# Queries loaded two tokens to a partition and turned by 64x64 identity products: attention followed by a hierarchical mixture of experts

## The chip, the cores and the metric

The kernel runs on one core of a Trainium2 chip. A core has TensorE for matrix products, VectorE (DVE) and ScalarE (ACT) for elementwise work, GpSimd (POOL), and SyncE (SP), which here only issues transfers. Transfers are issued on the queues of SP, ACT and POOL and are carried out by 16 DMA engines. The metric is the device time of one execution in microseconds (us).

## The reference

Queries have 8 batches of 16 heads, 384 tokens and 64 dimensions; keys and values have one head per batch. Every token's attention output, 16 heads x 64, is a row of 1024 that goes to one expert out of 4 groups x 4 experts.

```python
scores = (1/8) * q @ k.T
attn = softmax(scores); attn_out = attn @ v          # [B, H, S, D]
x = attn_out.transpose(0, 2, 1, 3).reshape(B * S, H * D)
g_idx = argmax(x @ w_group); g_w = softmax(x @ w_group)[g_idx]
e_idx = argmax(x @ w_expert[g_idx]); e_w = softmax(...)[e_idx]
out = g_w * e_w * (relu(x @ w1[g_idx, e_idx]) @ w2[g_idx, e_idx])
```

## The kernel before

Attention is done in 24 pairs `p`, three for each batch: a pair is one batch and one stretch of 128 tokens, for all 16 heads. For a pair the queries must stand as `qT`, a tile of 128 partitions x 1024: partitions 64a to 64a + 63 hold the 64 dimensions of the heads 8a to 8a + 7, and the columns are those eight heads by 128 tokens. The keys of a batch stand as `kT`, dimensions on partitions (in both halves) by 384 keys.

Scores are made in six rounds `j` of 64 keys (`scores`, L251): four float32 products on 64x64 tiles of the array, rows 64a (head half) by columns 64c (which four heads of the half), each 512 columns wide. ScalarE takes the exponential of a round (L253), VectorE adds the six rounds up (`pre_add`, L259 and L261) and folds them (L265) for the sums over keys, and `values` (L290) multiplies the exponentials with the batch's values, again in six rounds on four tiles. `weigh` (L300) multiplies with the inverse sums and leaves `xT`. At pair 2 the gate products of batch 0 (`gate_a`, L312) read `xT` of pair 0 and the choice of expert weights follows. From pair 4 on, the products with the chosen experts (L407, L415) are put between the rounds of attention.

The order of all work on each engine is the order in which the program is written. An engine takes its instructions in that order, and waits for semaphores. A transfer that is issued as the ninth or later waits for the landing of an earlier one, since eight semaphores go round.

Most pairs get their `qT` from a block transpose on VectorE (`prep_q`, L243), for which the queries are loaded in 128-byte pieces. The first four pairs (batch 0, and the first stretch of batch 1) get it otherwise. Their queries are loaded in natural order (`load_first`, tiles `qn` and `qe`): token on the partition, for each head one piece of 64 numbers, 256 bytes. `turn_q` then transposes them on TensorE: eight transposes of 128x128, one for each head position, both head halves side by side, into the space `qps`, from where they are copied to `qT`. For pair 0 the eight are two lots of four with a space each: ScalarE copies the first lot, VectorE the second. Pair 1 is turned after the first round of scores of pair 0 and copied by VectorE; pair 2 in pair 1, pair 3 in pair 2, both copied by ScalarE. The keys of batch 0 are loaded twice side by side (tile `kn`, both on ACT's queue), and turned by three transposes (`turn_k_first`, L219).

Ahead of all that 48 products of ones (L152, L442) keep TensorE busy while the first loads are on their way.

The loads at the start, in the order of their queues. ACT: keys twice, one quarter of pair 0's queries, then the table load and a first exponential (L160). SP: three quarters of pair 0's queries (L127), pair 1's in two loads (L129), batch 1's keys in four (L107), batch 0's values in two (L113), pair 2's queries in two (L134), pair 3's in two (L138), ten loads of gate weights (L199, L201), and batch 1's other queries (L92).

Of the kernel before, what the change touches and what calls it, by code (L numbers as in the profile page):

```python
# [9 lines left out]
FP32 = mybir.dt.float32  # L10
# [3 lines left out]
P = 128  # L14
# [7 lines left out]
def kernel(  # L22
# [11 lines left out]
    nc = tc.nc  # L34
    B, H, S, D = q.shape
# [6 lines left out]
    ST = S // P  # L42
# [5 lines left out]
    CW = 512  # L48
# [10 lines left out]
    HP = H // 2  # L59
    HC = CW // P  # L60
    NB = S // 32
    NBP = 2 * CW // 32
    KB = S // D
# [7 lines left out]
    pool = fast.enter_context(tc.tile_pool(name="work", bufs=2))  # L71
# [4 lines left out]
    def side(shape, dtype, name):  # L76
        return ps_s.tile(shape, dtype, tag="s", name=name)

    q_raw, k_raw, v_sb, kT, qT, pt, xT, xbf, gsel, wts = {}, {}, {}, {}, {}, {}, {}, {}, {}, {}

    q_todo = []
    q_nat = []
# [20 lines left out]
    def load_k(b):  # L103
        kt = pool.tile([P, NB, 32], FP32, tag="k", bufs=2, name="k")
        for a in range(2):
            for j in range(2):
                nc.sync.dma_start(out=kt[64 * a + 32 * j:64 * a + 32 * j + 32], in_=kv[b, 0, j])  # L107
        k_raw[b] = kt

    def load_v(b):  # L110
        vt = pool.tile([P, KB, D], FP32, tag="v", name="v")
        for c in range(2):
            nc.sync.dma_start(out=vt[64 * c:64 * c + 64], in_=v[b, 0].rearrange("(j i) d -> i j d", j=KB))  # L113
        v_sb[b] = vt

    qn = q[0].rearrange("(a hp) (st p) d -> st p a hp d", a=2, p=P)
    kn = k[0, 0].rearrange("(st p) d -> p st d", p=P)

    def load_first():
        kt = pool.tile([P, ST, 2, D], FP32, tag="k", bufs=2, name="kn")  # L120
        qt = pool.tile([P, ST, HP, 2, D], FP32, tag="qraw", bufs=2, name="qn")
        for a in range(2):
            nc.scalar.dma_start(out=kt[:, :, a], in_=kn)
        for c in range(2):
            hs = slice(c * HC, (c + 1) * HC)
            for a in range(2):
                (nc.scalar if c and a else nc.sync).dma_start(out=qt[:, 0, hs, a], in_=qn[0, :, a, hs])  # L127
        for a in range(2):
            nc.sync.dma_start(out=qt[:, 1, :, a], in_=qn[1, :, a])  # L129
        k_raw[0], q_raw[0] = kt, qt  # L130
        load_k(1)
        load_v(0)
        for a in range(2):
            nc.sync.dma_start(out=qt[:, 2, :, a], in_=qn[2, :, a])  # L134
        qe_in = q[1].rearrange("(a hp) (st p) d -> st p a hp d", a=2, p=P)
        qe = pool.tile([P, HP, 2, D], FP32, tag="y", bufs=4, name="qe")
        for a in range(2):
            nc.sync.dma_start(out=qe[:, :, a], in_=qe_in[0, :, a])  # L138
        q_nat.append(qe)

    def load_w1(w1, e):
# [11 lines left out]
    ident = singles.tile([P, P], FP32, name="ident")  # L153
    make_identity(nc, ident)
    load_first()

    one = singles.tile([P, 1], FP32, name="one")
# [38 lines left out]
    def load_gw():  # L196
        for a in range(2):
            rows = slice(a * D, (a + 1) * D)
            nc.sync.dma_start(out=gw[rows, :, 0:G], in_=moe_w_group.rearrange("(a ko d) g -> a d ko g", a=2, d=D)[a])  # L199
            for g in range(G):  # L200
                nc.sync.dma_start(out=gw[rows, :, G + g * Eg:G + (g + 1) * Eg], in_=moe_w_expert[g].rearrange("(a ko d) e -> a d ko e", a=2, d=D)[a])  # L201
# [13 lines left out]
    def turn_k_first():  # L215
        kT[0] = pool.tile([P, S], FP32, tag="kT", name="kT")
        ps = side([P, CW], FP32, "kps")
        for st in range(ST):
            nc.tensor.transpose(out=ps[:, st * P:(st + 1) * P], in_=k_raw[0][:, st].rearrange("p a d -> p (a d)"), identity=ident[:])  # L219
        nc.vector.tensor_copy(out=kT[0][:], in_=ps[:, 0:S])  # L220

    def turn_q(p, nat, copies):
        qT[p] = pool.tile([P, 2 * CW], FP32, tag="qT", bufs=2, name="qT")
        n = HP // len(copies)
        for i, copy in enumerate(copies):
            ps = side([P, 2 * CW], FP32, "qps")
            for h in range(n):
                nc.tensor.transpose(out=ps[:, h * P:(h + 1) * P], in_=nat(i * n + h).rearrange("p a d -> p (a d)"), identity=ident[:])
            copy(out=qT[p][:, i * n * P:(i + 1) * n * P], in_=ps[:, 0:n * P])

    def prep_k(b):
        kT[b] = pool.tile([P, S], FP32, tag="kT", name="kT")
# [2 lines left out]
    def q_of(p):  # L235
        b, st = divmod(p, ST)
        if b == 0:
            return q_raw[0][:, st].rearrange("p h a d -> p h (a d)")
        return q_raw[b][:, :, st * (P // 32):(st + 1) * (P // 32)].rearrange("p h k d -> p h (k d)")

    def prep_q(p):
# [91 lines left out]
    def counts(now, full):  # L333
        n = GE * (1 + ST)
        ps = side([P, n], FP32, "cps")
        lo, hi = (0 if now is not None else GE), (n if full is not None else GE)
        if now is not None:
            nc.tensor.matmul(out=ps[:, 0:GE], lhsT=ones_bf[:], rhs=first[now][:].rearrange("p g e -> p (g e)"), start=True, stop=True)
        if full is not None:
            nc.tensor.matmul(out=ps[:, GE:n], lhsT=ones_bf[:], rhs=ohe_t[full][:].rearrange("p s g e -> p (s g e)"), start=True, stop=True)  # L340
        t = pool.tile([P, n], FP32, tag="cnt1", bufs=2, name="cnt1")
        nc.scalar.copy(out=t[:, lo:hi], in_=ps[:, lo:hi])
        if now is not None:
            seen[now] = t[:, 0:GE]
            choose_b(now, t[:, 0:GE])
        if full is not None:
            gate_c(full, t[:, GE:n])
# [93 lines left out]
    for _ in range(18):  # L441
        nc.tensor.matmul(out=warm[:, 0:P], lhsT=ones_bf[:], rhs=ones_bf[:], start=True, stop=True)  # L442
    turn_k_first()
    turn_q(0, lambda h: q_raw[0][:, 0, h], [nc.scalar.copy, nc.vector.tensor_copy])
    load_gw()

    units = []
# [18 lines left out]
    def gates(b):  # L466
        if b == 0:
            choose_a(0, gate_a(0, 0, 1))
            return
        ps = gate_a(b, 0, ST)  # L470
        choose_a(b, ps)
        gate_logits(b - 1, ps, 1, ST)
        gate_math(b - 1)
# [72 lines left out]
    for p in range(NP):  # L546
        b, st = divmod(p, ST)
        jobs = [lambda: gates(0), lambda: None, lambda: counts(0, None)] if p == 2 else []
        if p == 0 or p == ST or (st == 1 and 1 < b < B - 1):
            load_q(b + 1)  # L550
        for j in range(3):
            scores(p, j)
            if p == 0 and j == 0:
                turn_q(1, lambda h: q_raw[0][:, 1, h], [nc.vector.tensor_copy])
        if p == 0:
            stats_k(0)
            prep_k(1)
        elif p == ST:
            prep_q(p + 1)
        if jobs:  # L560
            jobs.pop(0)()
        for j in (1, 2):
            pre_add(p, j)
        for j in range(KB):
            if p > 0:
                values(p - 1, j)
            if j == 2 and p > 0:
                join(p - 1)
            if j + 3 < KB:
                scores(p, j + 3)  # L570
            if 0 < j < 4:
                pre_add(p, j + 2)
            if j == 2 and p > 0:
                invert(p - 1)
            if j == 3:
                stats_q(p)
                if p == 1:
                    turn_q(2, lambda h: q_raw[0][:, 2, h], [nc.scalar.copy])
                elif p == 2:
                    turn_q(3, lambda h: q_nat[0][:, h], [nc.scalar.copy])  # L580
            if jobs:
                jobs.pop(0)()
            if p == ST + 1 and j == 0:
                fill(3)
            if st == 1 and 0 < b < B - 1 and j == 0:
                load_k(b + 1)
            if 0 < j < 5:
                some_q(1 if p <= ST + 1 else 2)
            if st == 1 and b + 1 < B and j == KB - 1:
                load_v(b + 1)  # L590
        assert not jobs
        if p > 0:
            weigh(p - 1)
        fold_keys(p)
        if st == 2 and b + 1 < B:
            stats_k(b + 1)
        if p in PHASES:
            n = PHASES[p]
            steps = {}
            if st < 2:  # L600
                prep_q(p + 1)
            if st == 0:
                counts(None, b - 2)
            elif st == 1:
# [258 lines left out]
```

## Time and profile before

| | |
|---|---|
| median of 5 runs | 463.21 us (462.59 to 463.55) |
| the profiled execution | 462.79 us, its span 461.3 us |
| mean granted clock of TensorE | 0.993 |
| busy, share of the span | TensorE 98%, VectorE 66%, ScalarE 53%, GpSimd 13% |
| 128x128 transposes of the queries (L228) | 32, of 273 ns each at the median, in four lots of eight |
| their copies to `qT` (L229) | ScalarE 0.59 us (half a pair) and 1.00; VectorE 0.69 (half a pair) and 1.22 |
| loads of the natural queries, issue to landing | pair 0's quarters 2.9 to 4.4 us, pairs 1 and 2 some 5 us, pair 3 5.4 us |

The span runs from the first to the last instruction; the execution's time has some 1.5 us around it. In the views below a row of the timeline has the start and duration in us, the engine, the source line, what is written and read, how many instructions were merged, and in brackets how long the engine stood idle before and what ended that. PEld is TensorE's loading of weights, PE its products. The rows of a view by windows have, for each stretch, its length and the busy time of PE, PEld, DVE, ACT and POOL with the number of instructions, then the granted clock as a share, the DMA engines' busy share and GB/s.

### The profile page before, as it was taken

The numbers are of one execution on the slowest core, as the hardware profiler recorded it, in microseconds if no ns is written. First come the engines' busy times: TensorE is split into PE (matmuls) and PEld (weight loads), VectorE is DVE, ScalarE is ACT, GpSimd is POOL, SyncE is SP. The second block draws the span as 40 slices with busy tenths as digits, with TensorE's granted clock in tenths as the row PEclk, the third lists the DMA queues.
The fourth block names the chain that finished last, engine by engine and source line by source line (L and its number), as shares of the span: only waits on it lengthen the run. The fifth ranks groups of instructions, "written<-read, shape, count | busy, mean of one in ns | idle before, by whom it ended". The sixth has DMA issues, their size and how long they took to land. (4 is left out here: it accounts for less than half of the span.)

```text
span 461.3 us, 10131 instructions
## 1 busy us (share of the span) xinstructions
PE 450.2 (98%) x4191; PEld 198.4 (43%) x4191; DVE 305.7 (66%) x483; ACT 242.6 (53%) x351; POOL 60.4 (13%) x83
## 2 busy tenths in 40 slices
PE   8999999999999999999999999999999999999992
PEld 6333444333533445343533435343443435344641
DVE  3899967954879286973779475992779564764400
ACT  2966645736366454646366364755457363623331
POOL 1004003000031002100030001300030000330000
PEclk9999999999999999999999999999999999999997
DMA  8788996998479691996759684996749712799991
GB/s 160 98 140 112 217 216 100 198 260 174 77 116 211 218 182 31 196 227 159 152 89 209 183 163 101 174 233 141 162 93 208 171 47 91 120 211 259 287 221 61
DMA packets 152165, 74.56 MB, mean 162 GB/s; under 512 B 120216, under 2 KB 138652, under 8 KB 152112
## 3 DMA queue, kind: packets, MB, share of 16 engines
q0 software_dynamic: 28416, 37.84, 47.6%
q1 hardware_dynamic: 122368, 35.68, 32.6%
q8 instruction: 35, 0.57, 0.5%
q10 hardware_dynamic: 1328, 0.33, 0.4%
q14 instruction: 18, 0.15, 0.1%
HBM read 92.62 MB, written 19.01 MB: 242 GB/s over the span
## 5 line engine op out<-in xcount | busy, mean ns | idle before, releaser
L253 ACT ACTIVATE pt<-s 128x1024 f32<-128x1024 f32 x144 | 142.1, 1026 | 67.7 <-PE s L251 66.9
L251 PE MATMUL s<-qT,kT 64*64 64x512 f32 x1152 | 143.0, 595 | 0.0
L290 PE MATMUL o<-pt,v 64*64 64x512 f32 x1152 | 141.0, 590 | 0.0
L261 DVE TENSOR_TENSOR presum<-presum,pt 128x1024 f32<-128x1024 f32 x96 | 116.6, 1215 | 16.3 <-ACT pt L253 10.9
L407 PE MATMUL hps<-xbf,w 128*128 128x384 bf16 x512 | 87.4, 326 | 0.0
L415 PE MATMUL yps<-w,hT 128*128 128x512 bf16 x384 | 85.4, 379 | 0.6 <-ACT y L416 0.6
L290 PEld LDWEIGHTS o<-pt,v 64*64 64x64 f32 x1152 | 43.5, 133 | 76.9 <-issue 73.2
L259 DVE TENSOR_TENSOR presum<-pt 128x1024 f32<-128x1024 f32 x24 | 29.4, 1224 | 69.3 <-ACT pt L253 68.5
L251 PEld LDWEIGHTS s<-qT,kT 64*64 64x64 f32 x1152 | 40.2, 133 | 64.3 <-issue 52.2
L416 ACT ACTIVATE y<-yps,gsel 128x512 f32<-128x512 f32 x48 | 32.6, 686 | 61.9 <-PE yps L415 49.9
L407 PEld LDWEIGHTS <-w 128*128 128x128 bf16 x512 | 48.5, 98 | 35.7 <-issue 4.1
L301 POOL CAST xbf<-xT 128x1024 bf16<-128x1024 f32 x24 | 25.0, 1041 | 280.4 <-DVE xT L300 280.4
L408 ACT ACTIVATE hT<-hps 128x384 bf16<-128x384 f32 x64 | 31.3, 488 | 50.8 <-PE hps L407 43.8
L415 PEld LDWEIGHTS <-hT 128*128 128x128 bf16 x384 | 36.8, 98 | 47.8 <-issue 4.9
L145 POOL DMA_DIRECT2D w<-in_moe_w_dram x36 | 24.8, 708 | 77.8 <-issue 58.7
L300 DVE TENSOR_TENSOR xT<-o,rinv 128x1024 f32<-128x1024 f32 x24 | 29.2, 1215 | 3.7 <-PE o L290 3.7
L280 DVE STREAM_TRANSPOSE rinv<-rc 128x1024 f32<-128x1024 f32 x24 | 29.9, 1245 | 0.8
L265 DVE TRANSPOSE_TENSOR_REDUCE fold<-presum 128x32 f32<-128x1024 f32 x24 | 29.6, 1232 | 0.0
L243 DVE STREAM_TRANSPOSE qT<-qraw 128x1024 f32<-128x1024 f32 x20 | 24.0, 1202 | 0.0
L209 ACT ACTIVATE qraw<-qraw 128x1024 f32<-128x1024 f32 x21 | 22.0, 1049 | 0.0
L318 DVE STREAM_TRANSPOSE L<-gps 128x32 f32<-128x32 f32 (+1 forms) x16 | 3.6, 227 | 17.4 <-PE gps L312 17.4
L273 PEld LDWEIGHTS sm<-fold,sel 64*64 64x64 f32 x192 | 7.2, 133 | 12.9 <-issue 12.9
(143 smaller groups left out, 156.3 us busy)
## 6 DMA issues: line engine op xcount, KB each, us to landing
w<-in_moe_w_dram POOLq DMA_DIRECT2D x36, 512.0 KB, 10.1
w<-in_moe_w_dram POOLq DMA_DIRECT2D x9, 2048.0 KB, 21.4
out_dram<-y SPq DMA_DIRECT2D x24, 512.0 KB, 2.8
qraw<-in_q_dram SPq DMA_DIRECT2D x56, 192.0 KB, 3.8
x_bf<-xbf SPq DMA_DIRECT2D x8, 768.0 KB, 4.5
v<-in_v_dram SPq DMA_DIRECT2D x16, 96.0 KB, 2.9
k<-in_k_dram SPq DMA_DIRECT2D x28, 48.0 KB, 2.6
qn<-in_q_dram SPq DMA_DIRECT2D x4, 256.0 KB, 5.0
```

Of the source, the lines that this page charges most:

```text
L251: nc.tensor.matmul(out=ps[64 * c:64 * c + 64, a, :], lhsT=kT[b][r, j * D:(j + 1) * D], rhs=qT[p][r, c * CW:(c + 1) * CW], start=True, stop ...
L253: nc.scalar.activation(out=t[:], in_=ps[:], func=ACTF.Exp, scale=scale)
L259: nc.vector.tensor_add(out=presum[p][:], in0=pt[p, 0][:], in1=pt[p, 1][:])
L261: nc.vector.tensor_add(out=presum[p][:], in0=presum[p][:], in1=pt[p, j][:])
L265: nc.vector.tensor_reduce(out=fold[p][:], in_=presum[p][:].rearrange("p a (n i) -> p (a n) i", i=32), axis=AX, op=OP.add, apply_transpose= ...
L280: nc.vector.transpose(out=t[:].rearrange("p (b i) -> p b i", i=32), in_=rc[:].rearrange("p c b -> p (c b)").unsqueeze(2).to_broadcast([P, ...
L290: nc.tensor.matmul(out=o_ps[p][64 * a:64 * a + 64, c, :], lhsT=v_sb[b][r, j, :], rhs=pt[p, j][r, a, :], start=(j == 0), stop=(j == KB - 1))
L300: nc.vector.tensor_mul(out=xT[b][:, :, ts], in0=o_ps[p][:].rearrange("p c (h n) -> p (c h) n", n=P), in1=rinv[p][:].rearrange("p (h n) -> ...
L407: nc.tensor.matmul(out=ps[:, 0:S], lhsT=w1[:, ko, fc * P:(fc + 1) * P], rhs=xb[:, ko, :], start=(ko == 0), stop=(ko == KO - 1))
L408: nc.scalar.activation(out=state["h"][:, fc, :], in_=ps[:, 0:S], func=ACTF.Relu)
L415: nc.tensor.matmul(out=ps[:], lhsT=state["h"][:, fo, st * P:(st + 1) * P], rhs=w2[:, fo, nh * CW:(nh + 1) * CW], start=(fo == 0), stop=(fo ...
L416: nc.scalar.activation(out=y, in_=ps[:], func=ACTF.Copy, scale=gs_of()[:, st:st + 1])
```

## The change

The queries of the first four pairs are loaded with two neighbouring tokens to a partition: `load_pairs` makes four loads for each pair, one for each c (which four heads of a half) and a (head half), of 64 partitions x 4 heads x 512 bytes; c picks the upper or lower 64 partitions. Pair 0's quarters go to SP, SP, SP, ACT, pair 1's to SP, SP, ACT, ACT, those of pairs 2 and 3 to SP.

`turn_q` multiplies each block of 64 token pairs x 64 dimensions with a 64x64 part of the identity: 32 float32 products for a pair in place of 8 transposes, on four tiles in turn (rows by c, columns by a). The result is written with a stride of two numbers, so that the tokens stand in order again. All 32 go to one space `qps` (the c halves in two banks); the copies are taken from there.

Batch 0's keys are loaded three tokens to a partition, and the values are loaded in the order that the turned keys then have, in four loads.

```diff
+    HQ = HP // 2
+    qn = q.rearrange("b (a c h) (st i t) d -> b st c a i h (t d)", a=2, c=2, st=ST, t=2)
+    kn = k[0, 0].rearrange("(p t) d -> p t d", t=ST)
+    vn = v[0, 0].rearrange("(u i t) d -> i t u d", u=2, t=ST)
+
+    def load_pairs(t, b, st, queues):
+        for c in range(2):
+            for a in range(2):
+                queues[2 * c + a].dma_start(out=t[64 * c:64 * c + 64, :, a].rearrange("p h t d -> p h (t d)"), in_=qn[b, st, c, a])
...
-        qt = pool.tile([P, ST, HP, 2, D], FP32, tag="qraw", bufs=2, name="qn")
+        qt = pool.tile([P, ST, HQ, 2, 2, D], FP32, tag="qraw", bufs=2, name="qn")
         for a in range(2):
             nc.scalar.dma_start(out=kt[:, :, a], in_=kn)
-        for c in range(2):
-            hs = slice(c * HC, (c + 1) * HC)
-            for a in range(2):
-                (nc.scalar if c and a else nc.sync).dma_start(out=qt[:, 0, hs, a], in_=qn[0, :, a, hs])
-        for a in range(2):
-            nc.sync.dma_start(out=qt[:, 1, :, a], in_=qn[1, :, a])
+        load_pairs(qt[:, 0], 0, 0, [nc.sync, nc.sync, nc.sync, nc.scalar])
+        load_pairs(qt[:, 1], 0, 1, [nc.sync, nc.sync, nc.scalar, nc.scalar])
         k_raw[0], q_raw[0] = kt, qt
         load_k(1)
-        load_v(0)
-        for a in range(2):
-            nc.sync.dma_start(out=qt[:, 2, :, a], in_=qn[2, :, a])
...
+        vt = pool.tile([P, KB, D], FP32, tag="v", name="v")
+        for c in range(2):
+            for u in range(2):
+                nc.sync.dma_start(out=vt[64 * c:64 * c + 64].rearrange("p (t u) d -> p t u d", u=2)[:, :, u], in_=vn[:, :, u])
+        v_sb[0] = vt
+        load_pairs(qt[:, 2], 0, 2, [nc.sync] * 4)
+        qe = pool.tile([P, HQ, 2, 2, D], FP32, tag="y", bufs=4, name="qe")
+        load_pairs(qe, 1, 0, [nc.sync] * 4)
...
     def turn_q(p, nat, copies):
         qT[p] = pool.tile([P, 2 * CW], FP32, tag="qT", bufs=2, name="qT")
-        n = HP // len(copies)
+        ps = side([P, 2, HQ, 64, 2], FP32, "qps")
+        for h in range(HQ):
+            for t in range(2):
+                for c in range(2):
+                    for a in range(2):
+                        r = slice(64 * c, 64 * c + 64)
+                        nc.tensor.matmul(out=ps[64 * a:64 * a + 64, c, h, :, t], lhsT=nat[r, h, a, t], rhs=ident[r, r], start=True, stop=True)
+        n = 2 * CW // len(copies)
         for i, copy in enumerate(copies):
-            ps = side([P, 2 * CW], FP32, "qps")
-            for h in range(n):
-                nc.tensor.transpose(out=ps[:, h * P:(h + 1) * P], in_=nat(i * n + h).rearrange("p a d -> p (a d)"), identity=ident[:])
-            copy(out=qT[p][:, i * n * P:(i + 1) * n * P], in_=ps[:, 0:n * P])
+            copy(out=qT[p][:, i * n:(i + 1) * n], in_=ps[:].rearrange("p c h i t -> p (c h i t)")[:, i * n:(i + 1) * n])
```

The four calls of `turn_q` hand over the tile itself where they handed over a function of the head; their places and copying engines stay. The order of instructions on every engine is otherwise the same.

More of the change, by code (lines that the diff above doesn't have):

```diff
@@ L114, in load_v @@
         v_sb[b] = vt
-    qn = q[0].rearrange("(a hp) (st p) d -> st p a hp d", a=2, p=P)
-    kn = k[0, 0].rearrange("(st p) d -> p st d", p=P)
+    HQ = HP // 2
[6 more added lines that the diff above has]
+                queues[2 * c + a].dma_start(out=t[64 * c:64 * c + 64, :, a].rearrange("p h t d -> p h (t d)"), in_=qn[b, st, c, a])
     def load_first():
         kt = pool.tile([P, ST, 2, D], FP32, tag="k", bufs=2, name="kn")
-        qt = pool.tile([P, ST, HP, 2, D], FP32, tag="qraw", bufs=2, name="qn")
+        qt = pool.tile([P, ST, HQ, 2, 2, D], FP32, tag="qraw", bufs=2, name="qn")
         for a in range(2):
             nc.scalar.dma_start(out=kt[:, :, a], in_=kn)
-        for c in range(2):
-            hs = slice(c * HC, (c + 1) * HC)
-            for a in range(2):
-                (nc.scalar if c and a else nc.sync).dma_start(out=qt[:, 0, hs, a], in_=qn[0, :, a, hs])
-        for a in range(2):
-            nc.sync.dma_start(out=qt[:, 1, :, a], in_=qn[1, :, a])
+        load_pairs(qt[:, 0], 0, 0, [nc.sync, nc.sync, nc.sync, nc.scalar])
+        load_pairs(qt[:, 1], 0, 1, [nc.sync, nc.sync, nc.scalar, nc.scalar])
         k_raw[0], q_raw[0] = kt, qt
         load_k(1)
-        load_v(0)
-        for a in range(2):
-            nc.sync.dma_start(out=qt[:, 2, :, a], in_=qn[2, :, a])
[L135 to L138, printed above, removed]
+        vt = pool.tile([P, KB, D], FP32, tag="v", name="v")
[6 more added lines that the diff above has]
+        load_pairs(qe, 1, 0, [nc.sync] * 4)
         q_nat.append(qe)
@@ L237, in q_of @@
         if b == 0:
-            return q_raw[0][:, st].rearrange("p h a d -> p h (a d)")
+            return q_raw[0][:, st].rearrange("p h a t d -> p h (a t d)")
         return q_raw[b][:, :, st * (P // 32):(st + 1) * (P // 32)].rearrange("p h k d -> p h (k d)")
@@ L443 @@
     turn_k_first()
-    turn_q(0, lambda h: q_raw[0][:, 0, h], [nc.scalar.copy, nc.vector.tensor_copy])
+    turn_q(0, q_raw[0][:, 0], [nc.scalar.copy, nc.vector.tensor_copy])
     load_gw()
@@ L553 @@
             if p == 0 and j == 0:
-                turn_q(1, lambda h: q_raw[0][:, 1, h], [nc.vector.tensor_copy])
+                turn_q(1, q_raw[0][:, 1], [nc.vector.tensor_copy])
         if p == 0:
@@ L577 @@
                 if p == 1:
-                    turn_q(2, lambda h: q_raw[0][:, 2, h], [nc.scalar.copy])
+                    turn_q(2, q_raw[0][:, 2], [nc.scalar.copy])
                 elif p == 2:
-                    turn_q(3, lambda h: q_nat[0][:, h], [nc.scalar.copy])
+                    turn_q(3, q_nat[0], [nc.scalar.copy])
             if jobs:
```

## The prediction

> **What bounds the kernel now.** I read the page first: its engine rows say that TensorE is busy for 98% of the 461.3 us span.
>
> ```profile
> PE 450.2 (98%) x4191; PEld 198.4 (43%) x4191; DVE 305.7 (66%) x483; ACT 242.6 (53%) x351; POOL 60.4 (13%) x83
> L251 PE MATMUL s<-qT,kT 64*64 64x512 f32 x1152 | 143.0, 595 | 0.0
> ```
>
> TensorE has no idle time to give back later, so what delays it at the start delays the end, unless a wait swallows it. Next the timeline of the first 30 us, since the change touches nothing later than pair 3's queries.
>
> ```profile
> 1.34 3.28 PE L152 MATMUL warm<-ones_bf 128*128 128x128 bf16 x30 [1.34 <-DVE one L158]
> 4.46 1.17 PE L442 MATMUL warm<-ones_bf 128*128 128x128 bf16 x18
> 5.46 0.50 PE L219 MATMUL kps<-ident,kn 128*128 128x128 f32 x3
> 6.43 0.59 ACT L229 COPY qT<-qps 128x512 f32<-128x512 f32 x1 [2.25 <-PE qps L228]
> 6.67 0.63 PE L228 MATMUL qps<-ident,qn 128*128 128x128 f32 x4 [0.28 <-DMA qn<-in_q_dram]
> 7.34 0.69 DVE L229 COPY qT<-qps 128x512 f32<-128x512 f32 x1 [0.79 <-PE qps L228]
> 8.08 0.20 PEld L251 LDWEIGHTS s<-qT,kT 64*64 64x64 f32 x4 [0.66 <-DVE qT L229]
> 9.21 1.02 ACT L253 ACTIVATE pt<-s 128x1024 f32<-128x1024 f32 x1 [2.19 <-PE s L251]
> 11.35 1.94 ACT L253 ACTIVATE pt<-s 128x1024 f32<-128x1024 f32 x2 [1.12 <-PE s L251]
> 12.41 1.23 DVE L259 TENSOR_TENSOR presum<-pt 128x1024 f32<-128x1024 f32 x1 [0.40 <-ACT pt L253]
> 13.74 5.21 DVE L261 TENSOR_TENSOR presum<-presum,pt 128x1024 f32<-128x1024 f32 x4
> 22.99 1.04 PE L290 MATMUL o<-pt,v 64*64 64x512 f32 x8
> 23.96 1.09 PE L228 MATMUL qps<-ident,qn 128*128 128x128 f32 x8
> 24.98 1.95 PE L290 MATMUL o<-pt,v 64*64 64x512 f32 x16
> 29.44 0.76 PE L312 MATMUL gps<-xT,gw 128*32 128x32 f32 x64
> ```
>
> The columns are start, duration, engine and line. One chain runs here: the query piece that lands last lets the second four transposes start (6.67), VectorE's copy follows (7.34), then the second half of the first scores (8.08), the first exponential (9.21), the second (11.35), and VectorE's first add (12.41). From that add VectorE has no gap in the timeline until the product xT ends at 29.34 (its row: 28.12, 1.22 long), which releases the gate matmuls at 29.44. So the second exponential sets the gate's time. TensorE itself is free at 29.33 (two rounds of scores from 27.61, four steps of 0.43), only 0.1 us earlier. From there to pair 3's turn TensorE leads: VectorE's row at 39.92 waits 0.65 us for it.
>
> **The change, part by part.**
>
> *Matmuls.* A pair is turned by 32 products on 64x64 tiles in place of 8 transposes on the whole array. A float32 product counts as two instructions in these rows (24 score products per pair, 1152 = 24 x 48), so 64 for 8. No row has 64 columns on such tiles. Per four instructions, one to each tile, the scores (512 columns) step by 0.43 us (24 in 2.75 us less 0.6 of flow, five steps), and the gate's 64 (32 columns) by 34 ns (weight-load row 0.65 us less 0.11, by 16). A straight line between gives 60 ns for 64 columns: 16 x 60 = 0.95 us a pair. Bounds: 34 ns gives 0.54, and the 109 ns step of a 128-column transpose gives 1.75. Now the turn takes more than its eight steps: pair 2's sits between values that leave the array at 23.85 (22.99 + 2 x 0.43) and values that start at 24.98, a slot of 1.13 us, with about 0.1 us lost on each side where whole-array and tiled work meet. With 0.95 the slot shrinks by 0.2 (by 0.6 at best, it grows by 0.6 at worst).
>
> The Trainium skill has this in "TensorEngine Tiling (Array Packing)", Key Properties: changing the tiling mode drains the array. The gaps above agree with it. It gives no number, and the sum goes by the slot.
>
> *Copies of pair 0.* Now ScalarE copies the first four heads' half while TensorE turns the second. Afterwards c is an inner loop, both halves are complete only after all 32 products, and VectorE's copy, in the program's order, waits for ScalarE's instead of for TensorE. Let T be the start of the turn that has all its data. Before: T 6.67 to the second score half 8.08, 1.41 us. After: 0.95 matmuls, 0.25 until the copy starts (now 0.31 from the last transpose, 0.05 of it column time), 0.59, 0.05 of hand-over, 0.69, 0.05: 2.58, less the last step of 0.06, so 2.52. This costs 1.11 us. If the copies ran side by side it would be 0.6 less.
>
> *Transfers.* Queries come in half as many pieces of 512 bytes. Now all 5519 packets between 2 and 8 us are under 512 bytes, at a mean of 219 GB/s. No load of 512-byte pieces is in the trace. Bounds: 220 GB/s (nothing gained), and 388 from the widest rows (x_bf's 768 KB land in 4.5 us, k's 48 KB in 2.6). I take 280, nearer to the 256-byte row. Keys (192 KB, still 256-byte pieces in the tile) take 0.89 us, and 640 KB of queries ahead of or beside the last piece of pair 0 (512 KB, and 128 KB of pair 1) 2.34. From the first packet at 2.2, with 0.8 from last packet to landing (k's 2.6 less 0.2 of data and some 1.6 of issue and start), the last lands at 6.2, T = 6.3 (now 6.67). Bounds: T = 6.95 at 220 GB/s, and 5.9 at 388, since the warming matmuls and the keys' transposes hold TensorE until then.
>
> The page "DMA: Bandwidth & Descriptors", Specifications, asks for at least 512 bytes for line rate. No row before shows such a load. With the 358 GB/s that it names per core, the queries would take 1.83 us and T would be at its floor of 5.9.
>
> *Pair 1's turn.* TensorE waits for its data until about 9.1 (loads issued at 2.62 and 3.2, 5.0 to 5.9 to landing). From score half to next load is 8.08 to 10.19, 2.11 us. Afterwards these pieces land well before 9, so 0.91 + 0.95 = 1.86: 0.25 less.
>
> *What is hidden.* SP issues 31 transfers ahead of the next batch's queries instead of 25, at 0.5 to 0.65 us each: up to 4 us later for all behind. The values are due at 17.49 and land at some 11.3 (issued by 8.4, 2.9 to landing); afterwards about 2 us later. The gate weights land by 22.6 (last issue at 19.9, 2.6), due at 29.44. Batch 1's queries land by 32 (28.1, 3.7), due at 42.2. Any cover lost costs its lateness one to one. On ScalarE's queue two more loads stand before the table load (1.28 us) and the wake (0.20). The last waits for the first keys' landing (1.02 + 3.1 = 4.1): 4.1 + 0.5 + 1.5 = 6.1, needed only at T + 1.1. Keys by three to a partition: the same three transposes and one copy; the values' order only follows. Statistics read the same elements in another order: 0.
>
> *Sum.* Score half at T + 2.52 = 8.82 (now 8.08): +0.74. Pair 1's turn -0.25: the second exponential, VectorE's chain and the gate come +0.5 late. Pair 2's 0.2 is lost there, since the gate waits for VectorE. Pair 3's turn (36.88, TensorE leads) gives -0.2. Together **+0.3 us**: span 461.6. The profiled execution took 462.79 in all (1.5 around its span), 0.42 under the median of 463.21. Added to the median: **463.5 us**. With T's bounds, -0.1 to +0.95.
>
> **Rivals.**
>
> *The clock falls (slower).* The first warming matmuls step by 109 ns, those at 4.46 by about 58: full clock comes after some 3 us of work. Near the end a stretch with TensorE busy for 1.75 of 3.40 us is followed by half clock:
>
> ```profile
> 451.50:454.90 3.40, 1.75 (x50) 1.00 (x42) 0.29 (x1) 0.86 (x2) 0.00 (x0) 1.00 0.38 143
> 454.90:458.30 3.40, 0.00 (x0) 0.00 (x0) 0.00 (x0) 0.00 (x0) 1.09 (x1) 0.51 0.13 37
> ```
>
> After the change TensorE waits about 0.4 us for data and then 1.4 us for the two copies, so a stretch of 3.4 us may be busy for only 45 to 59% (3.4 less 1.8 or less 1.4). Before, the same place (6 to 8 us) was busy for 1.72 of 2.00 us and kept its clock. If the limit lies above 55%, about 3.2 us run at half clock, which costs half of them: 463.5 + 1.6 = 465.1. Against it: idle time is less than half of any stretch but the worst placed.
>
> The skill's "TensorE: Matmul & The Clock Gate", What's actually happening, says that the clock falls after an idle window of about 3.4 us. A gap of 1.4 us would then cost nothing (463.5), but the row above fell after a half-busy one.
>
> *The tiles do not overlap (slower).* At 109 ns per four a turn takes 1.75, 0.8 more. Turns 0, 1 and 3 pay: +2.4, 465.9. Against: the gate's rows overlap four tiles.
>
> *The pieces land late (slower).* ScalarE's queue holds the keys and one piece of pair 0, beside 512-byte packets of SP that take the longer share of each turn. From T = 7.0 on it shows; at T = 7.3, +1.3, 464.5.
>
> *All goes well (faster).* T at 5.9 (-0.4) and three turns at 0.54 (-0.4 each): 0.3 - 1.6 = -1.3, 461.9. Against: a step of 34 ns was measured with half the columns.
>
> **How the numbers follow.** A difference under 0.2% (0.93 us) is about what a measurement of this kernel can tell from none. Forecast, near +0.3: 0.52. Clock 0.20, no overlap 0.08, late pieces 0.10: slower 0.38. Faster 0.10. The range takes in the forecast's own bounds (463.1 to 464.2) and reaches to the clock's case above and part of the good one below: 462.6 to 465.2.
>
> **What would show it.** The score half's load at 8.8, the second exponential at 11.85, the gate at 29.9. Turn products stepping by 60 ns per four. ScalarE's copy, then VectorE's, one after the other. A turn of pair 3 in a slot of 0.95. I am wrong if the granted clock falls at 8 to 13 us, if T is past 7, or if the gate moves by less than 0.2.

## The result and the profile after

| | before | after |
|---|---|---|
| median | 463.11 us (462.26 to 463.88, 49 runs) | 464.11 us (463.24 to 465.77, 29 runs) |
| ratio | | 1.0025, 95% interval 1.002 to 1.003 |
| profiled execution, its span | 462.79, 461.3 us | 464.77, 463.3 us |
| mean granted clock | 0.993 | 0.991 |

The changed kernel is slower, by 1.0 us of the medians and 1.2 by the ratio. The page of its profile has TensorE as full as before, and the scores at the same duration, so the time is in the places between:

```profile
PE 451.8 (98%) x4415; PEld 201.4 (43%) x4415; DVE 305.7 (66%) x483; ACT 242.6 (52%) x351; POOL 60.4 (13%) x83
L259 PE MATMUL s<-qT,kT 64*64 64x512 f32 x1152 | 143.0, 595 | 0.7 <-ACT qT L237 0.7
```

The timeline of its first 31 us, cut to the chain that the prediction followed (start, duration, engine, line, what is written and read, idle time before and its releaser):

```profile
4.51 2.13 PE L450 MATMUL warm<-ones_bf 128*128 128x128 bf16 x18
6.68 0.84 PE L223 MATMUL kps<-ident,kn 128*128 128x128 f32 x3
7.45 1.16 PE L234 MATMUL qps<-ident,qn 64*64 64x64 f32 x64
8.68 0.58 ACT L237 COPY qT<-qps 128x512 f32<-128x512 f32 x1 [2.78 <-PE qps L234]
9.30 0.69 DVE L237 COPY qT<-qps 128x512 f32<-128x512 f32 x1 [1.18 <-ACT qT L237]
10.04 0.19 PEld L259 LDWEIGHTS s<-qT,kT 64*64 64x64 f32 x4 [0.53 <-DVE qT L237]
11.16 1.02 ACT L261 ACTIVATE pt<-s 128x1024 f32<-128x1024 f32 x1 [1.90 <-PE s L259]
12.96 1.94 ACT L261 ACTIVATE pt<-s 128x1024 f32<-128x1024 f32 x2 [0.77 <-PE s L259]
14.01 1.22 DVE L267 TENSOR_TENSOR presum<-pt 128x1024 f32<-128x1024 f32 x1 [0.19 <-ACT pt L261]
24.60 1.04 PE L298 MATMUL o<-pt,v 64*64 64x512 f32 x8
25.46 1.11 PE L234 MATMUL qps<-ident,qn 64*64 64x64 f32 x64
26.39 1.90 PE L298 MATMUL o<-pt,v 64*64 64x512 f32 x16
29.73 1.22 DVE L308 TENSOR_TENSOR xT<-o,rinv 128x1024 f32<-128x1024 f32 x1
```

Each row answers to one of before. The turn of pair 0 has all its data at 7.45 (before 6.67), the second score half is loaded at 10.04 (8.08), the second exponential is at 12.96 (11.35), the first add at 14.01 (12.41), `xT` of pair 0 at 29.73 (28.12). So 1.6 us of delay are made before 14 us and none is given back up to `xT`. Pair 3's turn then gives 0.27 back (`xT` of pair 1 is at 41.26, before 39.92: +1.34).

Three of these rows show something else besides the change. The 18 warming products take 2.13 us, 1.17 before, and the keys' three transposes 0.84, 0.50 before: in this execution the granted clock rose at 7.36 us by the trace's record of it, in the profiled execution of before at 4.38. At the end the clock falls sooner, too. The view by windows has it (length, busy time of PE, PEld, DVE, ACT, POOL, clock, DMA share, GB/s):

```profile
451.50:454.90 3.40, 2.01 (x55) 1.34 (x55) 0.71 (x2) 0.74 (x2) 0.00 (x0) 0.94 0.38 154
```

The clock is 0.94 here (before 1.00): it fell at 454.50, and the last 32 products of the tail take 1.89 us (before 1.06). That is the larger part of why the two profiled executions lie 2.0 us apart in span, and the medians only 1.0. The rise comes at another place in each profile of this record, so the sizes below are read from two profiles in which it came early.

### The profile page after: what moved, and what is told of

Same layout as the page of the kernel before. It is cut to its first block, busy times and chain, and to the rows that moved or that the text cites. A ratio compares the mean times of both kernels' runs of the same rounds, so it can differ in the third digit from the quotient of the medians.

```text
span 463.3 us, 10584 instructions
## 1 busy us (share of the span) xinstructions
PE 451.8 (98%) x4415; PEld 201.4 (43%) x4415; DVE 305.7 (66%) x483; ACT 242.6 (52%) x351; POOL 60.4 (13%) x83
```

## The experiments

Twelve kernels, each timed beside the kernel before on the same chip. "Landing" is the time at which the last of pair 0's four pieces has landed; "T" is the prediction's, the start of the products that have all their data; both in us from the start of the span.

| kernel | median | ratio to before (95%) | landing | first add |
|---|---|---|---|---|
| before | 463.1 | | 6.58 | 12.41 |
| after | 464.11 | 1.0025 (1.002 to 1.003) | 7.31 | 14.01 |
| e1, two spaces | 463.33 | 1.0004 (0.9994 to 1.0013) | 6.98 | 13.02 |
| e2, tile turn alone | 462.30 | 0.9984 (0.9975 to 0.9993) | 6.74 | 12.96 |
| e3, half loads alone | 464.06 | 1.0018 (1.0009 to 1.0028) | 7.63 | 13.86 |
| e4, pair 1 on SP | 463.89 | 1.0018 (1.0008 to 1.0028) | 6.61 | 13.32 |
| e5, half loads, pair 1 on SP | 463.53 | 1.0012 (1.0003 to 1.0021) | 6.84 | 13.07 |
| e6, keys as before | 463.83 | 1.0017 (1.0005 to 1.0029) | 6.90 | 13.48 |
| e8, e1 and e4 | 463.33 | 1.0009 (0.9999 to 1.0018) | 7.04 | 13.08 |
| e9, before, 38 warming | 462.83 | 0.9994 (0.9985 to 1.0003) | 6.52 | 12.27 |
| e7, e2, 38 warming | 462.50 | 0.9990 (0.9981 to 0.9998) | 6.76 | 12.23 |
| e10, after, 38 warming | 463.94 | 1.0021 (1.0009 to 1.0032) | 6.96 | 13.53 |
| e11, key on GpSimd's queue | 463.82 | 1.0024 (1.0013 to 1.0035) | 6.92 | 13.55 |
| e12, e2, key on GpSimd's queue | 462.79 | 0.9993 (0.9984 to 1.0002) | 6.51 | 12.72 |

The theory was that two things cost the time: the copies of pair 0 in series, as predicted, and its pieces landing late, which the prediction had the other way round. The rivals were the products themselves, the keys' part, and the clock.

**e1: the changed kernel, pair 0's halves in two PSUM spaces.**

```diff
-        ps = side([P, 2, HQ, 64, 2], FP32, "qps")
+        two = len(copies) == 2
+        pss = [side([P, HQ, 64, 2], FP32, "qps") for _ in range(2)] if two else None
+        ps = None if two else side([P, 2, HQ, 64, 2], FP32, "qps")
...
+            for i, copy in enumerate(copies):
+                copy(out=qT[p][:, i * CW:(i + 1) * CW], in_=pss[i][:].rearrange("p h i t -> p (h i t)"))
```

> The changed kernel with the two halves of pair 0's turn in two spaces of their own, so that VectorE's copy waits for TensorE and not for ScalarE's copy. Theory 'series of copies': both copies start within 0.1 us of each other, and the second score half is loaded about 1.95 us after the start of the turn instead of 2.59; the time falls by 0.6 us against the changed kernel, to about +0.4 us over the kernel before. Rival 'it all hangs on the transfers': the copies are hidden behind something that ends later, the time stays at about +1.0 us over the kernel before. Rival 'the two engines disturb each other': each copy takes over 0.9 us instead of 0.59 and 0.69, and the gain is under 0.3 us.

The timeline of e1 has the two copies side by side:

```profile
7.11 1.15 PE L237 MATMUL qps<-ident,qn 64*64 64x64 f32 x60 [0.61 <-DMA qn<-in_q_dram]
8.21 0.59 ACT L240 COPY qT<-qps 128x512 f32<-128x512 f32 x1 [2.31 <-PE qps L237]
8.30 0.69 DVE L240 COPY qT<-qps 128x512 f32<-128x512 f32 x1 [1.46 <-PE qps L237]
```

VectorE's copy now waits for TensorE (L237), where after it waited for ScalarE's copy. The median falls by 0.78 us to that of before. The copies in series are a cost of the change, and most of it in the median. (The two were not timed side by side; each against its own series of the kernel before, the loss falls from 1.0 to 0.3 us, and the two ratios' intervals don't meet.)

**e2: the kernel before, pairs 1 to 3 turned by 64x64 products; loads, pair 0 and keys as before.**

```diff
     def turn_q(p, nat, copies):
...
+        if p > 0:
+            ps = side([P, 2, HP, 64], FP32, "qps")
+            for h in range(HP):
+                for c in range(2):
+                    for a in range(2):
+                        r = slice(64 * c, 64 * c + 64)
+                        nc.tensor.matmul(out=ps[64 * a:64 * a + 64, c, h, :], lhsT=nat(h)[r, a], rhs=ident[r, r], start=True, stop=True)
+            copies[0](out=qT[p][:].rearrange("p (h c i) -> p c h i", c=2, i=64), in_=ps[:])
+            return
```

> The kernel before, all loads as they were, with only the turn of pairs 1, 2 and 3 made by 64x64 products on four tiles (32 for each pair, token halves as rows). Theory 'the tile turn is a gain': a turn takes 16 x 58 ns = 0.93 us and its slot between values shrinks from 1.18 to about 0.92; pair 3's gain reaches the end, pair 1's does as far as its data is there: 0.3 to 0.5 us faster than the kernel before. Rival 'no slot is saved, waits fill it': within 0.1 us of before. Rival 'it costs': the four loads of each quarter row make it slower by 0.3 us or more.

462.30, 0.7 us faster than before (0.3 to 1.2 by the interval), and the interval ends below 1. The products are the part of the change that pays, and they need none of the new loads: a token half of a tile in natural order is as good a block for them.

**e3: the kernel before, with the queries of pairs 0 and 1 in loads of 64 partitions on the queues of the changed kernel, 256-byte pieces.**

```diff
-        for c in range(2):
-            hs = slice(c * HC, (c + 1) * HC)
-            for a in range(2):
-                (nc.scalar if c and a else nc.sync).dma_start(out=qt[:, 0, hs, a], in_=qn[0, :, a, hs])
-        for a in range(2):
-            nc.sync.dma_start(out=qt[:, 1, :, a], in_=qn[1, :, a])
+        for st in range(2):
+            for c in range(2):
+                r = slice(64 * c, 64 * c + 64)
+                for a in range(2):
+                    (nc.scalar if c and (a or st) else nc.sync).dma_start(out=qt[r, st, :, a], in_=qn[st, r, a])
```

> The kernel before, with the eight loads of pairs 0 and 1 in the shape and on the queues of the changed kernel (64 partitions each, four loads a pair, three of the last four on ACT's queue or behind a wait), but with 256-byte pieces and one token to a partition. Theory 'shape and number of transfers': an issue takes 0.6 us or more instead of 0.45 to 0.5, pair 0's last piece lands after 7.1 us as in the changed kernel (7.3; before 6.6), and the kernel is 0.4 to 1.0 us slower than before. Rival 'the 512-byte pieces are slow': pieces of 256 bytes land by 6.7 us, and the time is within 0.3 us of before.

464.06: the new shape and queues of the loads, with the old turns and copies and the old size of a piece, are slower than before by 0.8 us (the ratio) to 1.0 (the medians). Pair 0's last piece lands 1.05 us later than before. But not all of the loss is the landing. A piece is now a stretch of 64 tokens and no longer a group of heads, so each of the eight 128x128 transposes needs all four pieces, and none runs ahead of the last one:

```profile
7.77 1.07 PE L227 MATMUL qps<-ident,qn 128*128 128x128 f32 x8 [0.54 <-DMA qn<-in_q_dram]
9.62 0.20 PEld L250 LDWEIGHTS s<-qT,kT 64*64 64x64 f32 x4 [0.35 <-DVE qT L228]
```

From T to the second score half it is 1.85 us here, where before, with four transposes done and ScalarE's copy begun ahead of T, it is 1.41: 0.44 us that come with the shape at any landing.

**e4: the changed kernel, pair 1's loads all on SP's queue.**

```diff
-        load_pairs(qt[:, 1], 0, 1, [nc.sync, nc.sync, nc.scalar, nc.scalar])
+        load_pairs(qt[:, 1], 0, 1, [nc.sync] * 4)
```

> The changed kernel with pair 1's four loads all on SP's queue, behind pair 0's, and none on ACT's. Theory 'pair 1's data is moved ahead of pair 0's': pair 0's last piece lands at 6.7 us or earlier instead of 7.3, the turn starts 0.5 us or more earlier, and the time is 0.4 to 0.7 us under the changed kernel's. Rival 'shape and number of transfers': SP's issues are no shorter, the last piece still lands after 7.0, and the time stays within 0.2 us of the changed kernel's.

In the profiled execution the last piece lands at 6.61, 0.7 before that of the changed kernel; the median falls by 0.2 only, which the intervals don't tell from nothing. The turn started at 6.75 in that execution, behind warming products at half clock and the keys, so its early landing could not show in full.

**e5: e3 with pair 1's loads all on SP's queue.**

```diff
-                    (nc.scalar if c and (a or st) else nc.sync).dma_start(out=qt[r, st, :, a], in_=qn[st, r, a])
+                    (nc.scalar if c and a and not st else nc.sync).dma_start(out=qt[r, st, :, a], in_=qn[st, r, a])
```

> The kernel before with pair 0's and pair 1's queries in loads of 64 partitions and 256-byte pieces, pair 1's all on SP's queue; turns and copies as before. Theory A, pair 1's loads on ScalarE's queue are what makes pair 0's last piece late: it lands at 6.6 to 6.8 us (before 6.58, the same shape with ScalarE's queue shared 7.63), second exponential at 11.4 to 11.6, median 463.0 to 463.3. Theory B, the shape of the load (64 partitions, longer issues, later first data) makes it late on any queue: landing at 7.1 or later, second exponential at 12.0 or later, median 463.7 to 464.2. Beside the changed kernel with pair 1 on SP (512-byte pieces, landing 6.61) it also shows the size of a piece: if 512 bytes are worth something, this one lands 0.3 or more after it.

463.53, between the two theories: the landing (6.84) is nearly A's, the second exponential (12.01) is B's. The turn starts at 6.97, 0.30 later than before, and from T to the second score half it is 1.85 us, as in e3: the 0.44 of the shape are here too. With the queue e3's median falls by 0.5 us (464.06 to 463.53), on another chip, and the intervals of the two ratios overlap, so the queue's share isn't shown. A part stays with the shape (1.0012, its interval above 1). In the landing the size of a piece decides nothing that shows: it is 6.84 here, 6.61 in e4 and 7.04 in e8, whose query loads are e4's.

**e6: the changed kernel, keys and values loaded as before.**

```diff
-    kn = k[0, 0].rearrange("(p t) d -> p t d", t=ST)
+    kn = k[0, 0].rearrange("(st p) d -> p st d", p=P)
...
+        load_v(0)
```

> The changed kernel with the first batch's keys and values loaded as before, in natural order; queries loaded and turned as in the changed kernel. Theory: the keys' part moves nothing, since TensorE gets to the keys' transposes only after the warming products: median 463.9 to 464.3, exponentials within 0.2 us of those of the changed kernel at the same rise of the clock. Rival: the three-to-a-partition keys or the values in four loads hold up the queries behind them; then the last piece of pair 0 lands 0.3 us or more earlier than 7.31, and the median falls to 463.6 or less.

463.83, just under the theory's band and over the rival's. The landing is 0.4 us sooner than in the changed kernel, as the rival has it, but e10, with the changed kernel's loads, lands at 6.96, and the second exponential (12.42) gains nothing on that of e11 (12.49) at about the same rise of the clock. One thing is plain in the trace: the keys' first load takes 0.44 us to issue here and 0.67 in the changed kernel, and the first packet comes at 2.13 in place of 2.48. What that is worth, up to 0.3 us, the runs don't tell from nothing.

**e8: e1 and e4 together.**

> The changed kernel with pair 0's halves in two PSUM spaces and pair 1's loads all on SP. Theory A, series copies and late pieces are two separate costs and their mends add: landing 6.6, second score half at T + 1.95 = 8.7, second exponential 11.5, median 462.8 to 463.2, no slower than the kernel before. Theory B, an earlier landing is worth nothing, because the warming products and the keys hold TensorE to 6.7 or later in most executions: median 463.2 to 463.5, as with the two spaces alone.

463.33, B's number. But its reason isn't B's: in the profile the last piece lands at 7.04 (SP's third, not ScalarE's) and the products wait for it, so that e4's early landing did not come back. The rise of the clock came at 6.38, and this execution was the slowest of its twelve. Loads that are the same land 0.4 us apart from one execution to the next.

**e9, e7 and e10: 38 warming products in place of 48, in the kernel before, in e2 and in the changed kernel.** Their edit is the same:

```diff
-    for _ in range(18):
+    for _ in range(8):
```

> The kernel before with 38 warming products in place of 48. Theory: in the executions whose clock rises late, the warming products step by 107 ns to their end and hold TensorE until 6.5 us instead of 5.45; ten fewer end at 5.4 even at half clock, so those executions come 0.5 to 1 us sooner and the others stay: median 462.4 to 462.9, highest run under 463.5. Rival: the late executions are late for their half-clock keys and turns, or for their data, not for the warming; then the median stays within 0.2 us of 463.1. Second rival: with less work the clock rises one window later more often; then some runs go past 464.

> The kernel before with pairs 1 to 3 turned by 64x64 products (loads unchanged) and with 38 warming products. If the two gains add (0.7 us of the turns, 0.3 to 0.7 of the warming): median 461.7 to 462.2, faster than before by 0.2% or more. If the warming is worth nothing: 462.3, as with the turns alone.

> The changed kernel with 38 warming products in place of 48. Theory: its loss to the kernel before is in the pieces' landing (about 7.0) and the copies in series, not in the warming, so it gains less than the kernel before does from the same edit: median 463.8 to 464.1. Rival: the changed kernel is slow because its warming more often runs at half clock; then it falls to within 0.2 us of the kernel before with 38.

e9: 462.83; its highest run (of 11) is 463.19, where that of before (of 29) is 464.26, as the theory has it, but the median's gain of 0.16 is not told from none. e7: 462.50, so the gains don't add; it is no better than e2. e10: 463.94, and its rival falls: the changed kernel does not lose its time to the warming.

e9 and e10 are the pair to read the change from, since the clock rose at 5.26 and 4.27, before the work on pair 0 in both. The timeline of e9, the kernel before with 38:

```profile
6.62 0.63 PE L228 MATMUL qps<-ident,qn 128*128 128x128 f32 x4 [0.36 <-DMA qn<-in_q_dram]
8.03 0.19 PEld L251 LDWEIGHTS s<-qT,kT 64*64 64x64 f32 x4 [0.66 <-DVE qT L229]
11.21 1.94 ACT L253 ACTIVATE pt<-s 128x1024 f32<-128x1024 f32 x2 [1.04 <-PE s L251]
27.98 1.21 DVE L300 TENSOR_TENSOR xT<-o,rinv 128x1024 f32<-128x1024 f32 x1
39.78 1.23 DVE L300 TENSOR_TENSOR xT<-o,rinv 128x1024 f32<-128x1024 f32 x1 [0.64 <-PE o L290]
```

The timeline of e10, the changed kernel with 38:

```profile
5.34 0.37 PE L234 MATMUL qps<-ident,qn 64*64 64x64 f32 x4
7.00 1.15 PE L234 MATMUL qps<-ident,qn 64*64 64x64 f32 x60 [1.29 <-DMA qn<-in_q_dram]
9.56 0.19 PEld L259 LDWEIGHTS s<-qT,kT 64*64 64x64 f32 x4 [0.53 <-DVE qT L237]
12.48 1.94 ACT L261 ACTIVATE pt<-s 128x1024 f32<-128x1024 f32 x2 [0.77 <-PE s L259]
29.25 1.21 DVE L308 TENSOR_TENSOR xT<-o,rinv 128x1024 f32<-128x1024 f32 x1
40.78 1.23 DVE L308 TENSOR_TENSOR xT<-o,rinv 128x1024 f32<-128x1024 f32 x1 [0.39 <-PE o L298]
```

TensorE stands ready at 5.7 and waits 1.29 us for a piece. T is 7.00 against 6.62, the second score half 9.56 against 8.03, the second exponential 12.48 against 11.21, `xT` of pair 1 40.78 against 39.78. From here the distance stays, up to `xT` of the last pair (415.97 against 414.97), and the medians differ by 463.94 - 462.83 = 1.11. The two profiled spans differ by 1.6, since 0.55 more arises behind TensorE's last product.

**e11: the changed kernel, the second copy of the keys on GpSimd's queue, and pair 0's third piece on ScalarE's in its place. e12: e2 with the same move of the key.**

```diff
-            nc.scalar.dma_start(out=kt[:, :, a], in_=kn)
-        load_pairs(qt[:, 0], 0, 0, [nc.sync, nc.sync, nc.sync, nc.scalar])
+            (nc.gpsimd if a else nc.scalar).dma_start(out=kt[:, :, a], in_=kn)
+        load_pairs(qt[:, 0], 0, 0, [nc.sync, nc.sync, nc.scalar, nc.scalar])
```

> The changed kernel with the second copy of the first keys loaded from GpSimd's queue, and pair 0's third piece from ScalarE's in place of SP's. Theory A, a piece lands some 3.65 us after its issue ends, and SP's third issue ends 0.74 later in the changed kernel than before because loads of 64 partitions take longer to issue: now the last issue of pair 0 ends near 3.0 instead of 3.32, its last piece lands near 6.65, and the second exponential comes 0.2 to 0.4 sooner than at the same clock (12.48 with 38 warming products): 12.1 to 12.3, median 463.6 to 463.9. Theory B, the amount of data in flight sets the landing: still 6.9 to 7.3, median 464.0 to 464.2. If GpSimd's queue brings the keys later than 6.3, the keys decide instead, and the median rises.

> The kernel before with pairs 1 to 3 turned by 64x64 products and the second copy of the first keys loaded from GpSimd's queue, so that pair 0's piece on ScalarE's queue is issued one load sooner. Theory A: its issue ends at 2.1 instead of 2.65 us, it lands near 6.0, SP's third (6.1 to 6.3) then decides, T falls by 0.3 and the median to 461.9 to 462.2. Theory B: the keys from GpSimd's queue land after 6.0 and hold the keys' transposes and the score: 462.4 or more.

e11: the last issue of pair 0 ended at 3.04 us in place of 3.32, and yet the piece landed at 6.92, the second exponential came at 12.49 and the median is 463.82, not told from the changed kernel. A's landing and exponential did not come, though the median lies in its range, and the keys and the warming products (the clock rose at 6.69) held TensorE to 6.99 in any case. In this execution the earlier end of the issue did not bring an earlier landing; with landings that spread by 0.4 us one profile shows no more than that. e12: ScalarE's piece lands at 5.43, but SP's third still at 6.51, and the key copy from GpSimd at 6.49, so that the keys' transposes start at 6.58, 0.81 us behind the last warming product (5.77). 462.79, as B had it.

What goes with the later landing shows in the view by windows. Before:

```profile
2.00:4.00 2.00, 2.00 (x22) 2.00 (x21) 1.81 (x11) 1.30 (x2) 0.43 (x3) 1.00 0.96 216
5.00:6.00 1.00, 1.00 (x17) 1.00 (x15) 0.01 (x1) 0.00 (x0) 0.00 (x0) 1.00 1.26 219
```

After:

```profile
2.00:4.00 2.00, 2.00 (x22) 2.00 (x21) 1.80 (x11) 0.00 (x0) 0.43 (x3) 1.00 0.62 151
5.00:6.00 1.00, 1.00 (x12) 1.00 (x10) 0.00 (x0) 0.88 (x2) 0.00 (x0) 1.00 1.11 259
```

And e10:

```profile
2.00:4.00 2.00, 2.00 (x22) 2.00 (x21) 1.81 (x11) 0.00 (x0) 0.43 (x3) 1.00 0.69 176
6.00:7.00 1.00, 0.00 (x0) 0.00 (x0) 0.01 (x1) 0.00 (x0) 0.00 (x0) 1.00 1.17 222
```

The last column is GB/s. From 2 to 4 us the changed kernel moves 151 (e10 176) where the kernel before moves 216: 80 to 130 KB less. Afterwards it moves little more than before does, 222 to 259. Added up from the trace's packets, from the first packet to the landing of pair 0's last piece:

| | first packet | moved by the landing | mean rate |
|---|---|---|---|
| 128 partitions, 256 bytes (before, e2, e7, e9, e12) | 2.13 to 2.14 us | 960 to 1007 KB | 219 to 228 GB/s |
| 64 partitions, 512 bytes (after, e1, e4, e6, e8, e10, e11) | 2.47 to 2.49, e6 2.13 | 927 to 1085 KB | 221 to 242 |
| 64 partitions, 256 bytes (e3, e5) | 2.13 | 941 and 1092 KB | 203 and 205 |

Pair 0 and the keys are 704 KB of it; the rest is pair 1's, which shares the way. The 512-byte pieces win back what the loads of 64 partitions lose, and little more. The flow starts later: SP's first packet, which is pair 0's, comes at 2.14 before, at 2.54 with loads of 64 partitions (e3, e6), and at 2.82 or later where the keys come three to a partition as well. Whether more of pair 1 comes first when it is on two queues isn't shown: 1085 KB had moved in after and 927 in e4, with pair 1 on SP alone, but 988 in e8, with e4's loads, and 986 and 998 in e1 and e10, with those of after.

## Why the prediction was right, and where it was off

The forecast was 463.5 us, no change that can be measured, with its own bounds from 463.1 to 464.2 and a range from 462.6 to 465.2; 464.11 lies at the top of the bounds, and the difference now shows clear of noise. The forecast's middle has T moving the wrong way; it is the width of T's bounds that takes in the result. By the prediction's own sign of being wrong, T past 7, the profile of the changed kernel (7.45) is past it and e10 (7.00) stands on it. By its steps, with the sizes of e10 against e9:

| step | predicted | measured |
|---|---|---|
| T | -0.37 (6.67 to 6.3) | +0.38 (6.62 to 7.00) |
| T to the second score half | +1.11 (2.52 in all) | +1.15 (2.56) |
| pair 1's turn | -0.25 | -0.26 (from score half to second exponential, 3.18 to 2.92) |
| pair 2's turn | hidden | hidden (first add +1.26, `xT` of pair 0 +1.27) |
| pair 3's turn | -0.2 | -0.27 |
| sum | +0.3 | +1.0 |

**The copies in series** cost what was said, and e1 shows it by taking the wait away: 7.11 to about 9.05, 1.95 in place of 2.56. The prediction's 0.6 for copies side by side is there. The other 0.54 of the 1.15 (1.95 against 1.41 before) stays in e1: all products but the first four instructions now wait for the last piece, where before four transposes ran and ScalarE's copy began ahead of it. No kernel here gives that head start back.

**The products.** 64 instructions in 16 steps: 58 ns per four, where 60 were drawn between two rows. The slot of pair 2's turn, from 24.60 + 0.86 to 26.39, is 0.93 (before 1.13); 0.95 was predicted. Pair 1's term came out in size, but its reason was in part another: in e9 pair 1's data is there at 8.72, before its turn at 9.03, so the 0.26 there are the products' and not the data's. The rival in which the tiles do not overlap falls with it.

**The transfers** are the step that failed: "I take 280, nearer to the 256-byte row" and "From the first packet at 2.2". The rate was 230 GB/s from the first packet at 2.48 to the landing, and SP's own packets began at 2.97 (2.82 in e10). The prediction's bound of 220 GB/s gave T = 6.95, and 7.00 is what e10 has; with that bound it worked out +0.95, and +1.0 is what the medians show. That it comes so near is in part luck: in e10 the first packet came 0.27 later than the 2.2 of the sum, and the rate, 228, was above 220. In the profiled execution T is 7.45, since there the half-clock keys held TensorE to then, with the piece landed at 7.31. So the mechanism was in the text and the wrong end was chosen: the row of 256-byte packets was the near one in size, and a mean over both ends gave it a gain that no load of pair 0's kind had shown.

**The late pieces**, the rival of 0.10, had the sign and nearly the size: T of 7.0 to 7.3, up to 464.5. It blamed ScalarE's queue, and that isn't what the traces show: in all six profiles that load pair 0 as the changed kernel does (after, e1, e4, e6, e8, e10) the last piece to land is SP's third, and ScalarE's is 0.3 to 0.7 us sooner (6.87 and 7.31 in after). What the runs do show is a cost of the shape (e5 over before, 1.0012), a part of it the lost head start.

**The clock** did not fall. The window of e10 from 6 to 7 us has no TensorE work at all and a clock of 1.00, and the products after it step at full speed. But the stretch that the rival feared, busy for 45 to 59% (47 by its own 1.8 us), did not come up. Counted in steps of 3.41 us from the rise of the clock, the two waits of e10 fall on either side of a border, at 62% and 80%; the view by windows has the two stretches, and one of 59% at the end of the changed kernel, which half clock followed:

```profile
4.27:7.68 3.41, 2.12 (x64) 1.78 (x65) 0.56 (x1) 1.49 (x2) 0.00 (x0) 1.00 1.15 236
7.68:11.09 3.41, 2.73 (x87) 1.72 (x80) 0.69 (x1) 0.99 (x2) 0.00 (x0) 1.00 0.69 114
451.09:454.50 3.41, 2.02 (x63) 1.45 (x63) 0.71 (x2) 1.07 (x2) 0.00 (x0) 1.00 0.38 154
```

So the rival was not put to the test. No limit comes out either: in e1 a stretch at the end with 53% (1.80 of 3.42 us) was followed by full clock. What the prediction did not see is that the clock's rise differs between executions, so that two single profiles can differ by more than the change (2.0 us of span against 1.0 of the medians).

**What was hidden** stayed hidden: from the first add (+1.60) to `xT` (+1.61) no new wait came, for values or queries, and e10's distance to e9 stays at 1.0 us to the last pair, so none came for the gate weights or the later queries.

Left open: why loads of 64 partitions start later, and how T's 0.38 splits between the late start and pair 1's share. Not tried were loads with 512 bytes on 128 partitions, and an order of the products that is done with one half of pair 0 before the last piece lands.

The lowest median here is that of e2, 462.30: the products without the loads.

## What to carry to other kernels

A change of several parts is worth splitting: here the new products gain 0.7 us alone by the median (some 0.5 by the steps of the trace, 0.26 and 0.27), and the loads that came with them and one shared space give back more than twice that. A turn that needs every piece has lost its head start, so how a load is cut decides what can begin before the last piece is there. When a half-tile copy is to run beside another, each half needs its own space, or the second waits for the first although its data is there. For a piece that is waited for, count all the bytes that are under way with it, and take the rate from the row that looks most like the new load.

## What the runs showed of the hardware

The rise of TensorE's clock is a matter of the execution. In the 14 profiles it came between 4.09 and 7.36 us (4.09 to 5.26 in the three with 38 warming products), and it fell 447.15, 450.56 or 453.97 us later: 131, 132 or 133 times 3.413. The Trainium skill, "TensorE: Matmul & The Clock Gate", What's actually happening, has a free-running window of 3413 ns behind the clock, and the multiples agree with it; it puts the spread of the rise at 0.5 us to either side, where these runs spread over 3.3.

Pieces of 512 bytes did not bring a higher rate than before. The skill's "DMA: Bandwidth & Descriptors", Specifications, asks for 512 bytes for line rate; here loads of 512-byte pieces ran at 221 to 242 GB/s, and loads of 256-byte pieces on twice as many partitions at 219 to 228. On the same 64 partitions 256-byte pieces ran at 203 and 205 (e3, e5), so the longer piece gains about what the fewer partitions lose.

A load of 64 partitions took its queue 0.59 to 0.83 us to issue, one of 128 partitions with the same 128 KB 0.45 to 0.58. The second load of the keys took 0.95 to issue on GpSimd's queue and landed 4.25 us (e11) and 4.72 us (e12) after its start. From ScalarE's queue, second in line, it was 3.50 to 3.81 with the loads of before (before, e2, e7, e9), so e12's is later than these; with the changed kernel's it was 2.93 to 4.82 (after, e1, e4, e8, e10), and e11's lies among them.
